# Mask weights of 128 columns, and filler products placed ahead of the evacuation of their bank, in a causal-attention and channel-mix kernel

## The chip, the cores and the metric

The kernel runs on one core of one Trainium2 chip. The metric is the device time of one execution in microseconds (us), and the median of the runs is compared. The engines are PE (TensorE, the matrix products; PEld is its weight loads, which overlap the products), DVE (VectorE), ACT (ScalarE), POOL (GpSimd) and SP, which issues the DMAs. PE reads weights and moving data from SBUF and writes to PSUM, which has eight banks. DVE and ACT read the results out of PSUM.

## The reference

Inputs are q, k and v for 4 batches and 12 heads, 448 positions, 64 values a head, and the weights of a channel mix.

```python
scores = scale * np.matmul(q, k.transpose(0, 1, 3, 2))
mask = np.triu(np.ones((seq, seq), dtype=bool), k=1)
scores = np.where(mask, -1000000000.0, scores)
scores = scores - np.max(scores, axis=-1, keepdims=True)
attn = np.exp(scores)
attn = attn / (np.sum(attn, axis=-1, keepdims=True) + 1e-09)
x = np.matmul(attn, v)                     # 12 heads side by side: 768 channels
...
xk = mu_k * x + (1.0 - mu_k) * x_prev      # x_prev: x one position back
xr = mu_r * x + (1.0 - mu_r) * x_prev
k = np.maximum(xk @ w_k, 0.0)              # 768 -> 1024
v = k * k @ w_v                            # 1024 -> 768
r = 1.0 / (1.0 + np.exp(-(xr @ w_r)))      # 768 -> 768
out = r * v
```

## The kernel before

**Tiling.** Two heads make a pair, and there are 24 pairs (w = 0 to 23), six in a batch. The 448 positions are cut into four chunks of 112. The scores of a pair are made in three groups (g = 0, 1, 2), and each group has one PSUM tile `s` of two banks, one bank for each head j. There are two such tiles (the ring `s`), so the scores of group g+2 wait until the exponentials of group g have been read out. The channel mix of a batch follows its six pairs: the products `mk` (with w_k), `mr` (with w_r) and `mv` (with w_v). The weights arrive from HBM during the first pairs and are taken apart into two halves on ACT, POOL and DVE (`wraw`, `wk`, `wr`, `wv`; lines L689, L699, L703).

**The mask as products.** In `score`, four small products (L381, a quartet: two column ranges h by two heads j) write the mask into the diagonal blocks before the score products (L394) add to it. Their weights are `pick`, a selection matrix of 64 rows by 112 columns for each h, their moving data is `mask`. Head j lies on partitions 64j to 64j+63 of both, so a product of j = 0 uses one half of the rows of PE's array and one of j = 1 the other half. A quartet has four weight loads of `pick`. There are 72 quartets, 288 mask products.

**The rest of a pair.** DVE takes the row maxima (`row_max`, L411; `row_top`, L425 or L423), ACT makes the exponentials (`exps`, L434), and in the first six pairs PE turns them (`turn_e`, L512, tiles `eT`) and DVE or ACT copies the turned blocks to SBUF (`copy_e`, L523, tiles `pT`). The `eT` tiles stand in the ring `s` for pairs 2 and 3 and in the ring `m` for pairs 0, 1, 4 and 5. The weighted sum (L554) goes into one PSUM tile `bank`, which is read by `evac` on DVE (L571), which multiplies it into `xt`. The row sums take a way of their own (`rs`, `rp`, `rt`, `sp`: L452, L459, L465, L469, L475, L485).

**The filler.** The function `idle` issues pairs of a weight load and a product that no result depends on (L277, weights `busy` of 128x128, 64 columns out). They are written into `spill`, the 64 columns of `bank` behind the 448 that hold the weighted sum, so that they share a tile with the reads of `evac`:

```python
bank = ps_x.tile([P, 512], F32, name="bank")
spill = bank[:, S:]
```

**The order.** Nothing is scheduled while the kernel runs. Every step is an `op` of a plan, and `Plan.run` issues all of them in the order of a table of numbers, `starts`. Each filler run is an entry `[number, pieces]` of the table `fills`, which is put among the steps by its number and issues twice as many products as it has pieces. An engine works through its own instructions in that order. A wait between engines is set where a later instruction of the order touches what an earlier one writes or reads: a filler issued behind an `evac` waits for that read, and an `evac` issued behind a filler waits for the filler.

Of the kernel before, what the change touches and what calls it, by code (L numbers as in the profile page):

```python
# [11 lines left out]
BF16 = mybir.dt.bfloat16  # L12
# [21 lines left out]
class Plan:  # L34
# [60 lines left out]
    "engines": "PPPPPPADADAAPPDADADADDPPDDDADDDDDDADAPDDDDDPAADADADADAADPPAAADDAAAADDDDPAADDADDADAPAADDDAADDPPPPPPDPDAPDDADDADDPADPDDPADPADPADAAADDADADDAAAADDADADADADADADDDDDADADDDADAPPDDDPDADDDADDDAAADAAPDPDADDDADDDADPDADADPDAPAADAAAPPAAAPDADAADPPDADPDDPDDAPPADAADADDDAAPDPPDPPPDDADDAAADAPDDAPADAAPAAPAPDAAADPPDAADADAADDDPADDDDADPPAAPDADAPPPPPADADAAAPADDDDPDPAAAAADAADDDAAAADADDDADADAPADADADAADADAAAAAAAPDDDAADDADADPPAADDADADDPAPAPADDPPPPDADDPDDDDDPPDDDDADDPPAAADDPAADDDDADADADDAPAAAPDDDADDDDDDDDDPDDPADADADPPPDDDADADDAAPDDDADPADAAAADADADDDDDADADDADDPADADPDADAPAAAAADAAAAAAAPADDAPDADDDPPAAAPAPAPPAADPPAADDDAPDDPPPPADPAPDDPDAAPDADDAPDADAPPDPDPDDDDADPPADDDDDPPPDPPDDAAAADPPADADPDAAPDPPPDDDAAADADDPDAPPADAAADDDDDADADAAADAPDDDDAPAPADDPDDADDD",  # L95
    "fills": [[5,12],[125,16],[295,12],[485,2],[1345,16],[1575,2],[1645,2],[1685,1],[2015,2],[2075,4],[2225,16],[2335,2],[2355,1],[2915,5]],
}
# [3 lines left out]
def tile_causal_attention_channel_mix(  # L101
# [10 lines left out]
    nc = tc.nc  # L112
    B, NPAIR, P, _, S = qk.shape
    D = P // 2
    DM, DFF = w_k.shape
    CP = 112
# [16 lines left out]
    const = ctx.enter_context(tc.tile_pool(name="const", bufs=1))  # L133
# [27 lines left out]
    def triangles(t, other, pattern, by, base, fill):  # L161
        for x, off in ((other, 0), (t, D)):
            nc.gpsimd.affine_select(
                out=x, in_=x, pattern=pattern, compare_op=ALU.is_ge,
                fill=fill, base=base - by * off, channel_multiplier=by,
            )

    pick = const.tile([P, 2, CP], BF16, name="pick")
    mask = const.tile([P, 2, 1, CP], BF16, name="mask")
    mask_up = parted(x_ts[-1][:, 1 : 1 + CP])  # L170
    cleared(pick, mask_up, mask)
    ident = const.tile([P, P], F32, name="ident")
    make_identity(nc, ident)
    triangles(mask, mask_up, [[D, 2], [0, 1], [-1, CP]], 1, 0, masked)
    nc.vector.tensor_copy(pick[:D, 0], ident[:D, :CP])
    nc.vector.tensor_copy(pick[D:, 0, :D], ident[D:, D:])
    nc.vector.tensor_copy(pick[:D, 1, D:], ident[:D, : CP - D])
    nc.vector.tensor_copy(pick[D:, 1, D:], ident[D:, D:CP])
    nc.vector.tensor_copy(mask[:D], mask_up[:D])  # L179
# [5 lines left out]
    for h in range(2):  # L185
# [5 lines left out]
            fill=1.0,  # L191
# [142 lines left out]
    def short(w):  # L334

        return CHOICE["short"][w] == "R"
# [30 lines left out]
    def score(w, g):  # L367

        s = ps_s.tile([P, 2, 512], F32, tag="s", name=f"s_{w}_{g}")
        sps[w, g] = s  # L370
        for h in (1, 0):
            for j in range(2):
                rows = slice(D * j, D * j + D)
                a = D * h
                if g == 0:
                    diagonal = s[:CP, j, :S].rearrange("p (a b) -> p a b", a=2)[:, :, a:CP]
                    fill = mask[rows, h, :, a:].to_broadcast([D, 2, CP - a])
                else:
                    (c,) = STEPS[g]
                    diagonal, fill = s[:CP, j, CP * c + a : CP * (c + 1)], mask[rows, h, 0, a:]  # L380
                nc.tensor.matmul(  # L381
                    diagonal, pick[rows, h], fill, start=h == 1, stop=False, skip_group_check=True
                )
        if short(w):
            hi, lo = qkh[w]
            products = [(hi, lo), (lo, hi), (hi, hi)]
        else:
            products = [(qkt[w], qkt[w])]
        for c, o in STEPS[g].items():
            n = CP * (c + 1)  # L390
            for i, (q_, k_) in enumerate(products):
                for j in range(2):
                    rows = slice(64 * j, 64 * j + 64)
                    nc.tensor.matmul(  # L394
                        s[:CP, j, o : o + n],
                        q_[rows, 0, c * CP : (c + 1) * CP],
                        k_[rows, 1, :n],
                        start=False,
                        stop=c == max(STEPS[g]) and i == len(products) - 1,
                        skip_group_check=True,  # L400
                    )
# [624 lines left out]
    def scores(w):  # L1026
        ts_, tu = ("st", w, 3), ("su", w, 2)
        if short(w):
            n = 2 * S
            raw, hi, lo = have["qk", w], ("qk", nexts("qk"), NQ), ("qk", nexts("qk"), NQ)  # L1030
            plan.op(copied(n), 0, qk_hi, (w,), [(raw, None, "r"), (hi, None, "w")], fast=True)
            plan.op(less(n), 0, qk_lo, (w,), [(raw, None, "r"), (hi, None, "r"), (lo, None, "w")], fast=True)
            parts = [(hi, None, "r"), (lo, None, "r")]
        else:
            parts = [(have["qk", w], None, "r")]
        for g, chunks in enumerate(STEPS):
            s = ("s", nexts("s"), NS)
            n = sum(CP * (c + 1) for c in chunks)
            plan.op(
                "PE", (3 if short(w) else 4) * n / 2.4 + (150 if g == 0 else 175), score, (w, g),  # L1040
                parts + [(s, None, "w")],
            )
            plan.op(
                "DVE", sum(dve(2 * CP * (c + 1)) for c in chunks) - 88 * (len(chunks) - 1), row_max, (w, g),
                [(s, None, "w"), (ts_, g, "w")],
            )
            plan.op({"ACT": 210, "DVE": 160}, 0, row_top, (w, g), [(s, None, "r"), (ts_, g, "w")])
            for c in chunks:
                for j in range(2):
                    te = ("e", 2 * w + j, NE)  # L1050
                    plan.op(
                        "ACT", scalar(CP * (c + 1), True, 1) + 85, exps, (w, g, j, c),
                        [(s, None, "r"), (ts_, g, "r"), (te, c, "w"), (tu, (j, c), "w")],
                    )
# [287 lines left out]
```

## Time and profile before

| | |
|---|---|
| three runs | 473.27, 475.01, 475.00 us, median 475.0 us |
| the profiled execution, time | 472.84 us |
| its span, first to last instruction | 471.1 us |
| PE busy | 458.3 us (97% of the span) |
| DVE, ACT, POOL busy | 355.7, 298.3, 169.6 us |
| mean granted clock of PE | 0.993 of full speed |

Times in the trace are counted from the start of the span. Between the span and the execution's time lie 1.7 us. Matmuls are pipelined and their ends are modelled, so the start of one matmul to the start of the next says more than the duration of either. The granted clock is given as a share: 1.00 is 2.4 GHz and 0.50 is 1.2 GHz.

### The profile page before, as it was taken

The page shows a single profiled execution, that of the slowest core. Times are in us where ns is not written, and L with a number is a line of the kernel's source. Part 1 is how long each engine was busy: PE and PEld are TensorE (multiplying, and loading weights), DVE is VectorE, ACT ScalarE, POOL GpSimd, SP SyncE. Part 2 cuts the span into 40 slices and gives each one's busy share as a digit, 9 for nine tenths or more (in the row PEclk, how much of TensorE's full clock was granted, in tenths as well). Part 3 has the DMA queues.
Part 4 walks back from the last instruction along what each step waited for, and adds up shares of the span by engine and source line. Part 5 has one row for each costly group of instructions (what it writes and reads, how often), then busy time and mean ns, then how long its engine had stood idle before and what let it go on. Part 6 is the DMA issues. An engine that isn't in the chain of part 4 may idle for free.

```text
span 471.1 us, 9420 instructions
## 1 busy us (share of the span) xinstructions
PE 458.3 (97%) x3565; PEld 268.0 (57%) x3565; DVE 355.7 (76%) x719; ACT 298.3 (63%) x821; POOL 169.6 (36%) x177
## 2 busy tenths in 40 slices
PE   8987999999999999999999999999999999999996
PEld 6655765554455656655566556555665655555553
DVE  5978799999898979989878999375689875434121
ACT  5978699999878958766657673655469543024200
POOL 4434354323121651353472343465413342124100
PEclk9989899999999999999999999999999999999999
DMA  8975575657046878183066399374155574000011
GB/s 309 323 285 202 180 248 174 186 210 176 0 101 120 185 135 157 60 212 92 1 118 139 87 168 213 76 173 88 34 95 109 105 131 129 1 0 1 0 61 58
DMA packets 94846, 60.59 MB, mean 129 GB/s; under 512 B 83408, under 2 KB 86480, under 8 KB 94032
## 3 DMA queue, kind: packets, MB, share of 16 engines
q1 hardware_dynamic: 94800, 59.98, 50.2%
q8 instruction: 28, 0.46, 0.4%
q14 instruction: 18, 0.15, 0.1%
HBM read 33.82 MB, written 5.51 MB: 83 GB/s over the span
## 4 chain that ended last, share of the span: by engine, by line
PE 80%; DVE 10%; ACT 4%; issue 2%; DMA 2%; POOL 1%; SPq 0%; DVEq 0%; ACTq 0%; POOLq 0%
PE mv L815 21%; PE mk L815 18%; PE mr L815 13%; PE s L394 7%; PE bank L554 6%; PE mk L830 4%; PE mr L830 3%; PE s L381 3%; DVE s L411 2%; PE eT L512 2%; ACT e L434 2%; DMA wraw<-in_w_k_dram 2%; PE sp L475 1%; DVE xr L598 1%; ACT junk L655 1%
## 5 line engine op out<-in xcount | busy, mean ns | idle before, releaser
L815 PE MATMUL mv<-k,wv 128*128 128x448 f16 x576 | 113.7, 353 | 0.0
L434 ACT ACTIVATE e<-s,st 112x336 f32<-112x336 f32 (+3 forms) x192 | 93.0, 493 | 21.4 <-DVE st L425 16.4
L815 PE MATMUL mk<-xk,wk 128*128 128x448 f16 x432 | 83.8, 353 | 0.0
L815 PEld LDWEIGHTS <-wv 128*128 128x128 f16 x576 | 54.7, 98 | 50.4 <-issue 2.0
L411 DVE TENSOR_REDUCE s<-s 112x2 f32<-112x224 f32 (+2 forms) x96 | 70.8, 745 | 12.3 <-PE s L394 9.3
L815 PEld LDWEIGHTS <-wk 128*128 128x128 f16 x486 | 46.6, 98 | 43.2 <-issue 1.2
L815 PE MATMUL mr<-xr,wr 128*128 128x448 f16 x270 | 55.2, 352 | 0.0
L815 PEld LDWEIGHTS <-wr 128*128 128x128 f16 x270 | 26.1, 99 | 23.2
L434 ACT ACTIVATION_READ_ACCUMULATOR e<-s,st 112x1 f32 x192 | 38.9, 203 | 0.0
L830 PE MATMUL mk<-xk,wk 128*128 128x448 f32 x96 | 37.7, 545 | 0.0
L925 DVE SCALAR_TENSOR_TENSOR a<-mv,kap,a 128x448 f32<-128x448 f32 x24 | 16.2, 680 | 26.8 <-PE mv L815 26.2
L492 DVE TENSOR_TENSOR p<-e,p 112x1120 f16<-112x1120 f32 x25 | 34.3, 1377 | 1.3 <-ACT p L488 1.2
L492 POOL TENSOR_TENSOR p<-e,p 112x1120 f16<-112x1120 f32 x11 | 26.7, 2430 | 18.8 <-ACT p L488 13.1
L554 PEld LDWEIGHTS <-vs 112*64 112x64 f16 x648 | 26.8, 110 | 6.2 <-issue 5.2
L830 PE MATMUL mr<-xr,wr 128*128 128x448 f32 x72 | 29.8, 550 | 0.0
L554 PE MATMUL bank<-pT,vs 112*64 112x224 f16 (+1 forms) x648 | 29.5, 245 | 0.0
L598 DVE SCALAR_TENSOR_TENSOR xf<-xt,shares,xf 128x448 f32<-128x448 f32 x36 | 25.1, 698 | 5.5 <-ACT xf L227 5.1
L699 POOL TENSOR_SCALAR wraw<-wraw 128x768 int32<-128x768 uint16 (+1 forms) x18 | 21.0, 1165 | 22.8 <-DMA wraw<-in_w_v_dram 12.5
L830 PEld LDWEIGHTS mk<-xk,wk 128*128 128x128 f32 x96 | 17.7, 190 | 16.9 <-issue 15.7
L838 ACT ACTIVATE a<-mk 128x448 f32<-128x448 f32 x18 | 9.8, 542 | 27.4 <-PE mk L815 26.3
L394 PE MATMUL s<-ql,qh 64*112 64x112 f32 (+3 forms) x144 | 25.7, 352 | 0.0
L381 PE MATMUL s<-mask,pick 64*112 64x48 bf16 (+3 forms) x288 | 22.9, 234 | 1.3 <-DVE mask L179 0.6
(219 smaller groups left out, 839.3 us busy)
## 6 DMA issues: line engine op xcount, KB each, us to landing
qk<-in_qk_dram SPq DMA_DIRECT2D x24, 448.0 KB, 4.0
wraw<-in_w_k_dram SPq DMA_DIRECT2D x6, 1024.0 KB, 8.5
wraw<-in_w_v_dram SPq DMA_DIRECT2D x8, 768.0 KB, 5.4
vraw<-in_v_dram SPq DMA_DIRECT2D x24, 224.0 KB, 4.6
out_dram<-a SPq DMA_DIRECT2D x24, 224.0 KB, 2.9
wraw<-in_w_r_dram SPq DMA_DIRECT2D x6, 768.0 KB, 4.4
pT<-p SPq DMA_TRANSPOSE x36, 4.7
muT<-in_mu_dram SPq DMA_DIRECT2D x1, 6.0 KB, 10.6
```

Of the source, the lines that this page charges most:

```text
L381: nc.tensor.matmul(diagonal, pick[rows, h], fill, start=h == 1, stop=False, skip_group_check=True)
L394: nc.tensor.matmul(s[:CP, j, o : o + n], q_[rows, 0, c * CP : (c + 1) * CP], k_[rows, 1, :n], start=False, stop=c == max(STEPS[g]) and i = ...
L411: nc.vector.tensor_reduce(most(w, g, c, c + 1), s[:CP, :, o : o + CP * (c + 1)], AX.X, ALU.max, negate=True)
L434: nc.scalar.activation(em[w, j][:, blocks(c)].rearrange("p a b -> p (a b)"), sps[w, g][:CP, j, o : o + CP * (c + 1)], AF.Exp, bias=stat[w] ...
L492: tt[e](p[:, NB:, :CP], em.pop((w, j)), p[:, :NB, :CP], ALU.subtract)
L554: nc.tensor.matmul(px[w][64 * j : 64 * j + 64, cols], value(j, vi), p(j, pi), start=n == 0 and i == 0, stop=last and i == len(steps) - 1, ...
L598: nc.vector.scalar_tensor_tensor(f, x_of(w)[:, :S], share(w, mu, 1), f, ALU.mult, ALU.add)
L699: nc.gpsimd.tensor_scalar(t, u, TOP3, -0.499, ALU.mult, ALU.add)
L815: nc.tensor.matmul(ps, w[:, wi, cols], x[:, xi, t0 : t0 + n], start=(i == 0 and a == 0), stop=(i == steps - 1 and a == 2),)
L830: nc.tensor.matmul(mps[m, kind, o][:, :n], z[:, o * P : (o + 1) * P], x, start=i == 0, stop=i == NO - 1)
L838: nc.scalar.activation(a, mps[m, "k", f][:, :n], AF.Relu)
L925: nc.vector.scalar_tensor_tensor(s, mps.pop((m, "v", o))[:, : M[m][2]], kap[m][:, 3:4], s, ALU.mult, ALU.mult)
```

## The change

The tile `pick` gets 128 columns in place of 112. The 16 new columns stay zero, so the mask products write 128 partitions of the scores in place of 112, and those 16 partitions are read by nobody. In `fills`, the run of 16 pieces at 1345 becomes one of 12 at 1245, the run of 16 pieces at 2225 is gone, and the last one has 3 pieces in place of 5: 44 filler products fewer, 142 in place of 186. `starts` and `engines` are the same. The number at the end of a tile's name differs between the two kernels, because names are counted as tiles are made.

```diff
-    "fills": [[5,12],[125,16],[295,12],[485,2],[1345,16],[1575,2],[1645,2],[1685,1],[2015,2],[2075,4],[2225,16],[2335,2],[2355,1],[2915,5]],
+    "fills": [[5,12],[125,16],[295,12],[485,2],[1245,12],[1575,2],[1645,2],[1685,1],[2015,2],[2075,4],[2335,2],[2355,1],[2915,3]],
...
-    pick = const.tile([P, 2, CP], BF16, name="pick")
+    pick = const.tile([P, 2, P], BF16, name="pick")
...
-    nc.vector.tensor_copy(pick[:D, 0], ident[:D, :CP])
+    nc.vector.tensor_copy(pick[:D, 0, :CP], ident[:D, :CP])
     nc.vector.tensor_copy(pick[D:, 0, :D], ident[D:, D:])
-    nc.vector.tensor_copy(pick[:D, 1, D:], ident[:D, : CP - D])
-    nc.vector.tensor_copy(pick[D:, 1, D:], ident[D:, D:CP])
+    nc.vector.tensor_copy(pick[:D, 1, D:CP], ident[:D, : CP - D])
+    nc.vector.tensor_copy(pick[D:, 1, D:CP], ident[D:, D:CP])
...
-                    diagonal = s[:CP, j, :S].rearrange("p (a b) -> p a b", a=2)[:, :, a:CP]
+                    diagonal = s[:, j, :S].rearrange("p (a b) -> p a b", a=2)[:, :, a:CP]
...
-                    diagonal, fill = s[:CP, j, CP * c + a : CP * (c + 1)], mask[rows, h, 0, a:]
+                    diagonal, fill = s[:, j, CP * c + a : CP * (c + 1)], mask[rows, h, 0, a:]
```

**First place.** These are PE's instructions of before around the run at 1345: the scores of group 1 of the fourth pair, a turned block, and the start of the filler run of 32 products, behind which the scores of group 2 (`s_2`) stand.

```order
L394 MATMUL s_1_524<-qk_434 112x336 x2
L512 MATMUL eT_1_2_535<-ident,e_1_344 112x112 [waits Activation_49]
L512 MATMUL eT_1_2_535<-ident,e_1_344 112x112 x3
L277 LDWEIGHTS busy
L277 MATMUL bank<-busy 128x64 [waits DVE_49]
```

These are PE's instructions of the changed kernel at the same place, ahead of a run of 24 products.

```order
L394 MATMUL s_1_524<-qk_434 112x336 x2
L512 MATMUL eT_1_2_535<-ident,e_1_344 112x112 [waits Activation_49]
L512 MATMUL eT_1_2_535<-ident,e_1_344 112x112 x3
L277 LDWEIGHTS busy
L277 MATMUL bank<-busy 128x64
```

On PE nothing has moved against its neighbours, since no step of PE stands between 1245 and 1345. The filler's wait for DVE is gone. On DVE the `evac` of that stretch (L571) stood without a wait before:

```order
L411 TENSOR_REDUCE s_1_524<-s_1_524 112x2 [waits PE_49,Activation_49]
L523 COPY pT_1_513<-eT_1_1_520 112x336
L425 TENSOR_SCALAR st_508<-s_1_524 112x2 [waits DVE_49]
L571 TENSOR_TENSOR xt_92<-bank,xt_92 128x448
L703 SCALAR_TENSOR_TENSOR wk<-wk,wraw_503 128x1024 [waits DMAHW2_49,Activation_49,Pool_49]
```

In the changed kernel DVE has the same rows, and the wait stands at the `evac`:

```order
L411 TENSOR_REDUCE s_1_524<-s_1_524 112x2 [waits PE_49,Activation_49]
L523 COPY pT_1_513<-eT_1_1_520 112x336
L425 TENSOR_SCALAR st_508<-s_1_524 112x2 [waits DVE_49]
L571 TENSOR_TENSOR xt_92<-bank,xt_92 128x448 [waits PE_49]
L703 SCALAR_TENSOR_TENSOR wk<-wk,wraw_503 128x1024 [waits DMAHW2_49,Activation_49,Pool_49]
```

The wait between filler and `evac` has changed its direction.

**Second place.** These are PE's instructions of before around the run at 2225: turned blocks of the fifth pair, the turned row sums `rp`, and the start of the second run of 32 products, behind which `eT_0_1_818` of the fourth pair stands.

```order
L512 MATMUL eT_0_0_768<-ident,e_0_706 112x112 x3
L512 MATMUL eT_0_1_774<-ident,e_0_706 112x112 x3
L465 LDWEIGHTS rs_136 [waits Pool_49]
L465 MATMUL rp_782<-identh,rs_136 128x112
L277 LDWEIGHTS busy
L277 MATMUL bank<-busy 128x64 [waits DVE_49]
```

In the changed kernel the next turned block of the fourth pair (`eT_0_1_778`) follows at once:

```order
L512 MATMUL eT_0_0_760<-ident,e_0_698 112x112 x3
L512 MATMUL eT_0_1_766<-ident,e_0_698 112x112 x3
L465 LDWEIGHTS rs_136 [waits Pool_49]
L465 MATMUL rp_774<-identh,rs_136 128x112
L512 MATMUL eT_0_1_778<-ident,e_0_517 112x112 [waits DVE_49,PE_49,Activation_49]
L512 MATMUL eT_0_1_778<-ident,e_0_517 112x112 x2
```

The wait for the `evac` is gone here with the run. No other engine has a row more or less, and apart from the filler PE has the same rows in the same order.

## Rows read from the trace of the kernel before

**Rows 1.** The page, part 1: busy time, share of the span, instructions.

```profile
PE 458.3 (97%) x3565; PEld 268.0 (57%) x3565; DVE 355.7 (76%) x719; ACT 298.3 (63%) x821; POOL 169.6 (36%) x177
```

**Rows 2.** Waits of PE over the span: us in total, times, longest.

```profile
PE bank L277 <- DVE xt L571: 4.9, 2, 2.9
...
PE bp_gm L260 <- DVE diag L256: 0.4, 1, 0.4
```

**Rows 3.** Timeline, first place: start, us, engine, line, shapes, count, [idle before].

```profile
25.40 0.59 PE L512 MATMUL eT<-ident,e 112*112 112x112 f32 x4
...
26.86 0.37 ACT L434 ACTIVATE e<-s,st 112x112 f32<-112x112 f32 x1
...
27.30 0.63 DVE L571 TENSOR_TENSOR xt<-bank,xt 128x448 f32<-128x448 f32 x1
...
27.83 1.23 DVE L703 SCALAR_TENSOR_TENSOR wk<-wk,wraw 128x1024 uint32<-128x1024 uint32 x1
...
27.98 1.87 PE L277 MATMUL bank<-busy 128*128 128x64 f16 x32 [1.99 <-DVE xt L571]
...
29.77 0.43 PE L381 MATMUL s<-mask,pick 64*112 64x48 bf16 x4
...
30.00 1.54 PE L394 MATMUL s<-qk 64*112 64x448 f32 x4
...
31.67 1.10 DVE L411 TENSOR_REDUCE s<-s 112x2 f32<-112x896 f32 x1 [2.62 <-PE s L394]
```

**Rows 4.** Timeline of PE at full clock: a filler run and a group 2 of scores.

```profile
10.70 0.86 PE L277 MATMUL bank<-busy 128*128 128x64 f16 x24
...
20.43 1.01 PE L394 MATMUL s<-qk 64*112 64x448 f32 x4
```

**Rows 5.** Windows: stretch, us, busy (count) of PE, PEld, DVE, ACT, POOL, clock, DMA, GB/s.

```profile
28.00:31.00 3.00, 3.00 (x40) 2.32 (x39) 1.06 (x1) 2.14 (x6) 1.83 (x1) 0.50 0.99 393
...
44.00:47.00 3.00, 0.15 (x6) 0.15 (x6) 2.80 (x3) 2.65 (x8) 1.70 (x2) 1.00 0.85 313
...
48.00:51.00 3.00, 3.00 (x26) 2.89 (x25) 2.57 (x5) 1.13 (x3) 0.00 (x0) 0.54 0.11 42
```

**Rows 6.** Timeline, second place.

```profile
44.55 0.63 ACT L434 ACTIVATE e<-s,st 112x448 f32<-112x448 f32 x1
...
46.18 0.61 DVE L571 TENSOR_TENSOR xt<-bank,xt 128x448 f32<-128x448 f32 x1
46.85 1.09 PE L277 MATMUL bank<-busy 128*128 128x64 f16 x32 [2.91 <-DVE xt L571]
...
48.29 2.09 DVE L523 COPY pT<-eT 112x336 f32<-112x336 f32 x4 [1.50 <-PE eT L512]
...
51.97 0.36 PE L381 MATMUL s<-mask,pick 64*112 64x96 bf16 x4
...
53.02 1.07 DVE L411 TENSOR_REDUCE s<-s 112x2 f32<-112x224 f32 x2 [1.26 <-PE s L394]
```

**Rows 7.** Groups of weight loads by form: busy us, mean ns, idle before.

```profile
L554 PEld LDWEIGHTS <-vs 112*64 112x64 f16 x648 | 26.8, 110 | 6.2 <-issue 5.2 <-ACT k L227 0.4 <-DVE k L902 0.4
...
L381 PEld LDWEIGHTS <-pick 64*112 64x112 bf16 x288 | 15.5, 128 | 14.7 <-issue 9.0 <-DVE st L425 0.7 <-PE mk L830 0.7
...
L475 PEld LDWEIGHTS <-sel 128*128 128x128 f16 x96 | 6.3, 100 | 5.1 <-issue 2.9
```

**Rows 8.** Timeline of PE, 199.04 to 199.05: into a quartet of masks.

```profile
198.74 0.35 PE L815 MATMUL mk<-xk,wk 128*128 128x448 f16 x1
199.02 0.25 PE L381 MATMUL s<-mask,pick 64*112 64x96 bf16 x2
```

**Rows 9.** Windows of line L381 alone in that quartet: PE, PEld, clock.

```profile
199.08:199.10 0.02, 0.02 (x2) 0.02 (x4) 1.00 0.00 0
199.10:199.12 0.02, 0.02 (x4) 0.02 (x4) 1.00 0.00 0
```

**Rows 10.** The chain that ended last: start, us, products of one kind.

```profile
192.28 6.81 PE mk L815 x36
```

## The prediction

> **What bounds the kernel now.** I read the page's busy times first, then what PE waits for, then the timeline of all engines around the two longest waits, the clock there, and last the weight loads and the products around one quartet of masks.
>
> PE is busy for 97% of the span [rows 1]. Busy time of PE is modelled, so this alone doesn't make PE the bound. The waits do: PE lost 4.9 us in two waits of its filler products for `evac`, and of what it waits for later than 58 us no entry is over 0.4 us [rows 2]. What makes PE earlier in the first 60 us therefore arrives at the end, as long as the engines that feed it become earlier too.
>
> At the first place PE is through with the turned block at 25.99 (25.40 and 0.59). The filler behind it waits until DVE has read `bank` at 27.93, runs 32 products to 29.77, and only then come the masks and scores of group 2 [rows 3]. DVE sits idle for 2.62 us until these scores are there [rows 3]. Meanwhile the granted clock has gone to 0.50, that is 1.2 GHz, after PE had stood still, and PE stays there from 28 to 31 us [rows 5]: the four score products take 1.54 us in place of 1.01 at 2.4 GHz [rows 3, 4].
>
> The second place is alike. The filler waits 2.91 us for the `evac` that ends at 46.79, the turned blocks behind it are late, DVE is idle for 1.50 us for them and for 1.26 us for the next scores [rows 6]. PE has stood still in most of 44 to 47, and from 48 to 51 the clock is 0.54 [rows 5]. In both places products that were to keep PE at work are what held it up.
>
> **First place, term 1.** Ahead of `evac` in the order, 24 filler products start at 25.99 and take 0.86 us [rows 3, 4], so they end near 26.9. That costs nothing, because the work that hides them is ACT's last exponential of group 0, which ends at 27.23 [rows 3] and frees the PSUM tile that `s_2` needs. Without that cover it would be 0.86 us. The new wait of `evac` for the filler is over at 26.9 too, ahead of the 27.30 at which DVE comes to it; behind it on DVE stand L703 and the row maximum, which would be delayed if the filler ended later. The masks of group 2 then start at about 27.3 in place of 29.77, 2.4 us earlier, and at 2.4 GHz the scores are through at about 28.5. DVE is at L703 until 29.06 (27.83 and 1.23), so its row maximum starts at 29.06 in place of 31.67: **2.6 us**. From here DVE, and not PE, hands on the gain, since exponentials and turned blocks follow from the row maximum. If the clock falls there as before, the scores are through at 29.1 and DVE's part stays the same, while the weighted sum behind them runs slowly until about 31: I estimate 1.9 us as the lower end. I take 2.6, since PE's idle time shrinks from 1.99 to about 0.4 us. The DMA engines are full from 28 to 31 us (0.99) [rows 5], so transfers under way can't land sooner; but none of these rows waits for a DMA, so I count no loss.
>
> **Second place, term 2** (in times of before; all of it comes 2.6 earlier). The turned block behind the removed run needs a PSUM tile that ACT frees at 45.18 (44.55 and 0.63), not the `evac` [rows 6]. So PE goes on at 45.3 in place of 47.9. DVE still has its `evac` until 46.79 and copies the block at once, at 46.85 in place of 48.29: 1.4 us on DVE. Copies on DVE and ACT then free the tiles one after the other for the rest of the turned blocks, which at 2.4 GHz brings PE to the next masks at about 49.4 in place of 51.97. DVE's next row maximum starts at 50.4 in place of 53.02, 2.6 us. If PE runs at 1.2 GHz here, as it did from 48 to 51, the turned blocks and row sums there take about a microsecond more, and 1.4 us are left. With the run gone, PE is at work for under half of this stretch, and it fell to 1.2 GHz once with the filler, so I take **2.1 us** between 1.4 and 2.6.
>
> The four products fewer of the last run are worth 4 times 28 ns, 0.1 us at most, since the run of 24 has 28 ns between starts (0.86 less the 0.2 of one product, over 23) [rows 4]. I count nothing for them: PE waits there for copies anyway.
>
> **Mask weights, term 3.** The load of `pick` with 112 columns takes 128 ns, one of 64 columns 110, but one of 128 columns (`sel`) takes 100 [rows 7]. The stream shows it more clearly: filler products with a 128-column load each start every 28 ns [rows 4], so such a load takes at most 28 ns of the stream. In the quartet at 199.02 the third mask starts between 199.10 and 199.12, 80 to 100 ns behind the first [rows 8, 9]. The masks ahead of it have 96 columns, 41 ns at the 189 ns that 448 columns take (6.81 us over 36) [rows 10]. Some 40 to 60 ns are the wait for the second pair of loads, and a load of 28 ns would save about 20 there and as much again ahead of the score products. I take 45 ns for a quartet. It counts only where PE comes from other work than scores, whose longer products hide the loads, and where PE is the bound: I choose 30 of the 72 quartets, **1.3 us**. The bounds: 72 times 60 ns is 4.3 us; and if the load isn't faster, 16 columns more at the 0.4 ns a column between 64 and 112 columns (18 ns over 48) [rows 7] are 6 ns a load, 1.8 us lost over 288. I take the gain because the nearest row (`sel`, the same width and element size) has it, though with 128 rows.
>
> The Trainium skill has a rule against this term: "TensorE: Matmul & The Clock Gate", section "LDWEIGHTS (loading the stationary operand)", has a load's time grow with its columns; its formula gives, as an estimate, 93 ns for 112 and 107 for 128. By that the change would cost 14 ns a load, 4 us in all if none were hidden. The trace doesn't agree, since its 128-column loads are the shorter ones. The same page, section "Weight-path perf modes — Fast Weight Load (FWL) and DoubleRow", says why: a fast load is used when the weights are exactly 128 columns and not FP32. No row here shows it for weights of 64 rows.
>
> **The sum.** 2.6 + 2.1 + 1.3 = 6.0 us. From the profiled execution, 472.84, that gives 466.8. The median of the runs is 475.0, 2.2 above it, with a lowest run of 473.27. I put the sum between, as the wait for a clock that falls now and then may be part of that spread: **468.0 us**.
>
> **The rivals.**
> (a) The waits go, but the mask loads gain nothing or lose: the short load isn't to be had with weights of 64 rows. For it speaks that no 64-row load of 128 columns stands in the trace. 1.3 to 3.1 us less gain: 469.5 to 471, the waits alone giving 4.7. By the skill's rule on columns it would come out here.
> (b) The early gain is lost again: DVE's copies and row maxima, or weights that arrive no sooner, hold PE by 60 us, and only half of term 1 is left with term 3, 2.6 us: 472.5 or, from the median without the clock's part, up to 474. For it speaks that DVE and ACT are nearly full in that stretch; against it that DVE itself had 5.4 us idle at these two places for PE, and its work moves along.
> (c) Slower: a short load of 128 columns takes all of PE's way for weights and can't stand beside a running product of the other half of the rows. On the switch from full products to half rows PE shows 0.28 us where 0.19 is normal, 94 ns of standing still [rows 8, 10]. Paid at each of 288 loads that is 27 us, 468 plus 28, about 496; it decides from 25 ns a load on, 7 us, which eats terms 1 and 2 and the margin. Against it: 28 ns a load and product in the filler.
> (d) More: 72 quartets gain 60 ns and the second place its 2.6 us, 3.5 us more: 464.5.
>
> **How the numbers follow.** Forecast 58%, with its own range of 466 to 470; (a) 20%; (b) 11%; (c) 5%; (d) 6%. The range of 464.5 to 472.0 holds forecast, (a) and (d) and leaves out (c) and most of (b). A change of under 0.5%, 2.4 us, can't be told from none here: faster means below 472.6. Forecast, (a) and (d) are faster, and a part of (b): 0.86. The rest of (b) is 0.09 with no change, (c) is 0.05 slower.
>
> **What would show it.** In the changed kernel's profile PE has no wait of L277 for L571 at 27 or 46 us; the filler run starts at 26.0 and the masks of group 2 at 27.3; DVE's row maximum comes at 29.1; the clock is 1.00 from 28 to 31. The masks that stood at 51.97 start at about 47. Loads of `pick` have a mean near 100 ns, and the third mask of a quartet starts 50 to 60 ns behind the first. It would be wrong if a wait of another engine stands where the filler waited, if the clock stays at 0.50 from 44 us on, if loads of `pick` are at 128 ns or more, or if mask to mask grows.

## The result, and the profile after

The changed kernel takes **468.38 us** in the median of 4 runs (466.07 to 469.34), against 475.0 us before (473.27 to 475.02): a ratio of 0.986, with an interval of 0.982 to 0.991. The profiled execution took 467.75 us, with a span of 466.0 us and a mean granted clock of 0.999. That is 5.1 us less than the profiled execution of before, 472.84. The forecast was 468.0.

The page's busy times, which answer to [rows 1], and what PE waits for, which answers to [rows 2]:

```profile
PE 452.7 (97%) x3521; PEld 260.7 (56%) x3521; DVE 355.6 (76%) x719; ACT 298.1 (64%) x821; POOL 169.6 (36%) x177
```

```profile
PE s L381 <- ACT e L434: 2.2, 3, 1.0
PE eT L512 <- ACT e L434: 2.2, 4, 1.3
PE bank L273 <- DVE busy L148: 1.1, 1, 1.1
PE s L381 <- DVE wz L703: 1.0, 1, 1.0
PE eT L512 <- DVE pT L523: 0.8, 1, 0.8
```

PE no longer has the entry of 4.9 us, the filler's waits for `evac`. New ones stand in the list, of 1.3, 1.0, 1.0 and 0.8 us. Those of 1.3 and 0.8 us stand at the second place, where PE now comes ahead of ACT and DVE; those of 1.0 us stand at 104 and 141 us. The one of 1.1 us (L273) is at the very start and stood there before.

The timeline of the first place, which answers to [rows 3]:

```profile
25.56 0.86 PE L277 MATMUL bank<-busy 128*128 128x64 f16 x24
...
27.28 0.25 PE L381 MATMUL s<-mask,pick 64*128 64x48 bf16 x4 [0.86 <-ACT e L434]
27.36 0.98 PE L394 MATMUL s<-qk 64*112 64x448 f32 x4
...
27.17 0.62 DVE L571 TENSOR_TENSOR xt<-bank,xt 128x448 f32<-128x448 f32 x1
27.70 1.23 DVE L703 SCALAR_TENSOR_TENSOR wk<-wk,wraw 128x1024 uint32<-128x1024 uint32 x1
28.84 1.10 DVE L411 TENSOR_REDUCE s<-s 112x2 f32<-112x896 f32 x1
```

The filler runs at once, the masks of group 2 wait 0.86 us for ACT's last exponential, and DVE goes from L703 to its row maximum without a pause. The second place, which answers to [rows 6]:

```profile
42.43 0.93 PE L512 MATMUL eT<-ident,e 112*112 112x112 f32 x7 [1.32 <-ACT e L434]
...
44.38 0.50 PE L512 MATMUL eT<-ident,e 112*112 112x112 f32 x3 [0.83 <-DVE pT L523]
...
46.32 0.31 PE L381 MATMUL s<-mask,pick 64*128 64x96 bf16 x4
...
43.30 0.61 DVE L571 TENSOR_TENSOR xt<-bank,xt 128x448 f32<-128x448 f32 x1
43.84 1.85 DVE L523 COPY pT<-eT 112x336 f32<-112x336 f32 x4
...
47.33 1.07 DVE L411 TENSOR_REDUCE s<-s 112x2 f32<-112x224 f32 x2 [0.27 <-PE s L394]
```

The masks that stood at 51.97 start at 46.32, and DVE's row maximum comes at 47.33 in place of 53.02. The windows of [rows 5] again, with busy times of PE, PEld, DVE, ACT and POOL, the granted clock, the DMA share and GB/s:

```profile
28.00:31.00 3.00, 2.84 (x30) 1.84 (x29) 3.00 (x7) 2.79 (x8) 2.22 (x3) 1.00 0.97 388
44.00:47.00 3.00, 2.62 (x32) 2.32 (x34) 3.00 (x8) 2.08 (x7) 0.00 (x0) 1.00 0.47 184
48.00:51.00 3.00, 3.00 (x36) 1.89 (x34) 2.71 (x6) 2.59 (x10) 2.86 (x3) 1.00 0.82 306
```

The clock stays at 1.00 in all three. The loads of `pick`, which answer to [rows 7], and the mask quartet that stood at 199.02, as in [rows 8, 9] (PE and PEld of line L381 alone, clock):

```profile
L381 PEld LDWEIGHTS <-pick 64*128 64x128 bf16 x288 | 9.7, 95 | 19.1 <-issue 12.1 <-DVE st L425 0.7 <-PE mk L830 0.7
```

```profile
194.75 0.31 PE L381 MATMUL s<-mask,pick 64*128 64x96 bf16 x4
```

```profile
194.78:194.80 0.02, 0.02 (x2) 0.02 (x4) 1.00 0.00 0
194.80:194.82 0.02, 0.02 (x4) 0.02 (x4) 1.00 0.00 0
```

A load of `pick` takes 95 ns where it took 128, and the third mask starts 50 to 70 ns behind the first, where it was 80 to 100.

**Where the time came from.** The start of the same instruction in both traces: the masks of [rows 3] come 2.49 us earlier (27.28 for 29.77; 0.22 of it was there at the quartet ahead, 24.33 for 24.55), those of [rows 6] 5.65 earlier (46.32 for 51.97), and a mask quartet later on 5.94 earlier (94.24 for 100.18). Then some of it goes: the quartet at 140.79 stood at 144.83, 4.04 earlier. At the end of the span it is 5.1 us. Two of these quartets in the trace of before, and the first of them in that of the changed kernel (the other is shown in the last section):

```profile
100.18 0.27 PE L381 MATMUL s<-mask,pick 64*112 64x48 bf16 x4
...
144.83 0.27 PE L381 MATMUL s<-mask,pick 64*112 64x48 bf16 x4
```

```profile
94.24 0.25 PE L381 MATMUL s<-mask,pick 64*128 64x48 bf16 x4
```

Below, the lead of a kernel at a quartet is the time by which its masks start there earlier than in the trace of before.

### The profile page after: what moved, and what is told of

The parts are those of the page before. It is cut to its first block, busy times and chain, and to the rows that moved or that the text cites. A ratio compares the mean times of both kernels' runs of the same rounds, so it can differ in the third digit from the quotient of the medians.

```text
span 466.0 us, 9334 instructions
## 1 busy us (share of the span) xinstructions
PE 452.7 (97%) x3521; PEld 260.7 (56%) x3521; DVE 355.6 (76%) x719; ACT 298.1 (64%) x821; POOL 169.6 (36%) x177
## 4 chain that ended last, share of the span: by engine, by line
PE 72%; DVE 10%; ACT 10%; issue 3%; DMA 3%; POOL 1%; ACTq 0%; DVEq 0%; SPq 0%
PE mv L815 20%; PE mk L815 18%; PE mr L815 13%; PE s L394 6%; PE bank L554 6%; PE mk L830 4%; ACT e L434 4%; DVE s L411 3%; DMA pT<-p 2%; PE s L381 2%; ACT junk L655 1%; PE mr L830 1%; PE eT L512 1%; PE sp L475 1%; DVE wv L733 1%
## 5 line engine op out<-in xcount | busy, mean ns | idle before, releaser
L434 ACT ACTIVATE e<-s,st 112x336 f32<-112x336 f32 (+3 forms) x192 | 93.1, 495 | 18.4 <-DVE st L425 11.2
L434 ACT ACTIVATION_READ_ACCUMULATOR e<-s,st 112x1 f32 x192 | 39.3, 205 | 0.0
L492 DVE TENSOR_TENSOR p<-e,p 112x1120 f16<-112x1120 f32 x25 | 35.1, 1406 | 2.4 <-ACT p L488 2.4
L492 POOL TENSOR_TENSOR p<-e,p 112x1120 f16<-112x1120 f32 x11 | 26.9, 2444 | 19.5 <-ACT p L488 10.8
L488 ACT CAST p<-e 112x1120 f16<-112x1120 f32 x19 | 21.4, 1127 | 5.2 <-DMA pT<-p 2.7
```

Of the source, the lines that this page charges most:

```text
L434: nc.scalar.activation(em[w, j][:, blocks(c)].rearrange("p a b -> p (a b)"), sps[w, g][:CP, j, o : o + CP * (c + 1)], AF.Exp, bias=stat[w] ...
L488: copy[e](p_t[at_][:, :NB, :CP], em[w, j])
L492: tt[e](p[:, NB:, :CP], em.pop((w, j)), p[:, :NB, :CP], ALU.subtract)
```

## The experiments

All ratios are to the kernel before, run on the same chip, where its medians were 474.3 to 474.7 us. A ratio is worked out over the runs and can be up to 0.0015 off the quotient of the two medians. Of each kernel with 112 columns `pick` is that of before.

**One half alone.** The weights of 128 columns with the old fills, and the new fills with the old weights; the diffs are the two halves of the one shown above.

> The kernel before with the 128-column weights of the masks and its own filler runs. Theory (the waits carry the gain, the mask loads add a little): 1.3 us faster, between 0.5 and 2.5 (ratio 0.995 to 0.999); the filler still waits 4.9 us for the two evacuations; loads of pick near 95 ns. Rival M (the mask loads carry most of it and the early gain is lost downstream): 4 us or more faster (0.992 or less).

Measured: 473.32 us, 0.9965 (0.9939 to 0.9991), as expected. In its trace the two waits are still there, 5.1 us in total, and a load of `pick` takes 95 ns.

> The kernel before with the new table of filler runs and 112-column weights. Theory: both waits gone, 5.6 us earlier at the first masks behind the second place, and 4 to 5.5 us faster at the end (0.988 to 0.9915). Rival N (what counts is that there are 44 products fewer): 1.2 us at 28 ns each, up to 2.5 us at the rate of 58 ns at 1.2 GHz. Rival M: 1 to 2 us.

Measured: 473.44 us, 0.9973 (0.9952 to 0.9994). That is 1.3 us where 4 to 5.5 were expected, and in the range of rival M. In its trace both waits are gone, but the masks behind the second place have a lead of 3.0 us (48.95), not of 5.6: 1.0 us was lost ahead of the first place, and the clock was at 0.51 from 46 to 49 us. The two halves add up to 0.994, the whole change was 0.986. Either the halves help each other, or one of these numbers doesn't stand for what it was taken to stand for.

**One place alone.** The first edit of `fills` alone, then the removed run alone.

```diff
-[1345,16],
+[1245,12],
```

> The kernel before with the first run alone put ahead of its evacuation (12 pieces at 1245 in place of 16 at 1345): 8 products fewer. Theory: 2.6 to 2.8 us earlier behind the first place, the second wait stays at about 2.9 us, and 2 to 2.8 us faster at the end. Rival N: 8 products, 0.2 to 0.5 us.

Measured: 472.89 us, 0.9970 (0.9942 to 0.9997).

```diff
-[2225,16],
```

> The kernel before with the second run alone taken out (16 pieces at 2225): 32 products fewer. Theory: first wait stays at about 2.0 us, 2.1 to 2.8 us earlier at the masks behind the second place, 1.5 to 2.8 us faster at the end, with the clock at 1.00 or falling there as the term assumed. Rival N: 32 products, 0.9 us at 28 ns to 1.9 us.

Measured: 473.67 us, 0.9973 (0.9951 to 0.9995). In both traces the place that was edited gives what the theory said: the lead grows by 2.5 us at the first place and by 2.2 at the second, both more than rival N allows. But both times fell by less than expected. The first kernel loses 1.4 us of its lead between 207 and 285 us, the second 2.5 between 72 and 79 and 2.0 between 144 and 199, more than it had gained. Two edits that by their ratios give 1.4 and 1.3 us alone, and 1.3 together, can't be read as a sum.

**The change a second time**, beside the next three kernels.

> The changed kernel once more, with more runs, beside the next three. The two halves alone gave 0.9965 and 0.9973, together 0.9938 if they add up, and the changed kernel gave 0.9862 with four runs. Theory A (they add up, and the four runs were good ones): 0.991 to 0.995. Theory B (the halves help each other: the early gain of the runs is lost later when mask loads are slow, and kept when they are short): 0.985 to 0.989.

Measured: 469.59 us (466.52 to 473.26), 0.9894 (0.9852 to 0.9936). That is just above the range of B, and 0.994 just outside the interval; over both measurements, 0.988, it is B's number. Whether the halves help each other, as B says, the times alone don't show. Its profiled execution was a long one, with a span of 471.5 us. These rows of its trace say where it lost, the windows with the same columns as above:

```profile
75.84 1.86 PE L830 MATMUL mk<-xk,wk 128*128 128x448 f32 x2 [2.17 <-DVE xk L598]
```

```profile
45.00:48.00 3.00, 3.00 (x26) 2.64 (x24) 2.19 (x6) 2.50 (x7) 0.56 (x2) 0.51 0.37 102
76.00:79.00 3.00, 3.00 (x12) 1.17 (x12) 2.93 (x6) 1.49 (x7) 1.83 (x2) 0.50 0.22 90
```

PE stood still for 2.17 us where the first execution of the same kernel had no wait, and twice the clock was at 0.50 where it had been 1.00. At the second place its lead grows by 1.5 us less than in the first execution, and around 76 us it loses another 3.9: together 5.4 of the 5.5 us between the two spans.

**Are the products fewer, or earlier?** All 186 products kept, with the three later runs ahead of the evacuations; then the changed kernel without the run at 1245.

```diff
-[1245,12],[1575,2],[1645,2],[1685,1],[2015,2],[2075,4],[2335,2],[2355,1],[2915,3]
+[1245,16],[1575,2],[1645,2],[1685,1],[2015,2],[2075,4],[2195,16],[2335,2],[2355,1],[2915,5]
```

> The changed kernel with all 186 filler products of before, both long runs ahead of their evacuations in the order (16 pieces at 1245, 16 at 2195, 5 at 2915). Theory (the waits carry the early gain, not the number of products): the masks behind the second place start within 0.6 us of the changed kernel's (46.3), and the time is within 0.4% of it. Rival N (the number of products): 44 products more cost 1.2 to 2.5 us there.

Measured: 467.82 us, 0.9866 (0.9828 to 0.9904). The time is as expected. The masks behind the second place start at 47.75, not within 0.6 us of 46.3 but 1.4 later; 1.3 of that was there ahead of the first place (25.63 for 24.33), and from there on the two differ by 0.1 us.

```diff
-[1245,12],
```

> The changed kernel without the run at 1245: 24 products fewer. Theory: they stood in time in which PE waits for ACT, so the scores of group 2 start at 27.3 as in the changed kernel and the early part is the same, unless the clock falls to 1.2 GHz behind 1.6 us of standing still, as it did before; then 0 to 1.5 us are lost by the masks at 46.3. Rival: fewer products are faster by themselves, 0.7 us.

Measured: 468.34 us, 0.9863 (0.9837 to 0.9888). As expected, the scores of group 2 start at 27.33, the masks behind the second place at 46.09, and the clock stays at 1.00. With all 186 products, 142 or 118 the time is the same within the intervals, about 2 us, and what the two places give differs by 0.1 and 0.3 us from the changed kernel: it is the place that counts there, not the number.

**Exactly 128?** The changed kernel with weights of 120 columns.

```diff
-    pick = const.tile([P, 2, P], BF16, name="pick")
+    pick = const.tile([P, 2, 120], BF16, name="pick")
...
-                    diagonal = s[:, j, :S].rearrange("p (a b) -> p a b", a=2)[:, :, a:CP]
+                    diagonal = s[:120, j, :S].rearrange("p (a b) -> p a b", a=2)[:, :, a:CP]
```

> The changed kernel with mask weights of 120 columns. Theory (exactly 128 columns make the load short): loads of pick at about 128 to 131 ns as with 112 columns, the third mask 75 to 90 ns behind the first, and 1 to 1.5 us slower than the changed kernel. Rival (more columns than 112 are enough, or the count of partitions written matters): loads near 97 ns and the same time.

Measured: 473.70 us, 0.9978 (0.9953 to 1.0003), the same as the new fills with 112 columns, and 4.1 us slower than the changed kernel beside it where 1 to 1.5 were expected. Its weight loads:

```profile
L381 PEld LDWEIGHTS <-pick 64*120 64x120 bf16 x288 | 16.2, 131 | 17.2 <-issue 12.0 <-PE mk L830 0.7 <-DVE wz L703 0.7
```

With 120 columns a load takes 131 ns, more than with 112 (128). Behind full products the third mask starts 83 ns after the first (the median of 16 quartets; 86 before, 52 in the changed kernel). Of the three widths tried, only 128 has the short load.

**Is the rest lost in collisions?** With the new fills and slow loads (112 or 120 columns), and in the changed kernel without the run at 1245, PE waited 1.2 us near 285 us. In the last one the timeline around it reads:

```profile
279.41 2.57 DVE L355 SCALAR_TENSOR_TENSOR vs<-vraw,vsc,vs 112x512 f16<-112x512 f32 x1
...
279.14 2.29 POOL L345 TENSOR_TENSOR ql<-qk,qh 128x896 fp32r<-128x896 f32 x1 [6.59 <-ACT qh L340]
...
282.57 0.21 PE L465 MATMUL rp<-identh,rs 112*128 112x112 f16 x1 [1.20 <-DVE xt L485]
```

DVE's L355 starts 0.27 us after GpSimd's L345 and takes 2.57 us in place of the 0.75 of the kernels without this wait. To take this away, the cast that releases GpSimd is put behind another one on ScalarE, in two kernels. On ACT, against the kernel without the run:

```order
-L340 CAST qh_3802<-qk_3593 128x896
-L605 CAST xk_3806<-xf_15_3716 128x448
+L605 CAST xk_3802<-xf_15_3716 128x448
+L340 CAST qh_3804<-qk_3593 128x896
```

> The new filler runs with the 112-column mask weights, and one more edit: on ScalarE the cast of xk at L605 stands ahead of the cast of qh at L340 where the kernel with the fills alone lost 1.2 us (PE waited there for DVE xt L485). In that kernel GpSimd's ql at L345 started 0.27 us ahead of VectorE's vs at L355, and that L355 took 2.57 us instead of 0.75. Theory C (collisions: what the two halves lack of the whole is lost later, in places where the engines that follow meet each other at a worse moment): L355 is back at 0.75 us, the wait of 1.2 us and the 0.4 us behind it are gone, and the time falls by 1.2 to 1.6 us against the fills alone, to a ratio of about 0.993 to 0.995 against the kernel before. Theory L (the 112-column loads themselves eat the gain, and any wait that is taken away comes back elsewhere): the ratio stays at 0.997.

> The change without its filler run at 1245, which showed the same stretched L355 (2.57 us) and the same wait of 1.2 us, with the same swap on ScalarE (L605 ahead of L340). Theory C: the wait goes, the time falls by 1.2 to 1.6 us, from a ratio of 0.986 to about 0.983, which would be the fastest version. Theory L: 0.986, since the wait comes back elsewhere.

Measured: 472.91 us, 0.9964 (0.9934 to 0.9994), and 468.82 us, 0.9878 (0.9834 to 0.9922). In the second one's trace:

```profile
281.82 0.74 DVE L355 SCALAR_TENSOR_TENSOR vs<-vraw,vsc,vs 112x512 f16<-112x512 f32 x1
...
284.57 1.46 DVE L609 TENSOR_TENSOR xk<-xf,xk 128x448 f16<-128x448 f32 x1
...
283.47 2.08 POOL L345 TENSOR_TENSOR ql<-qk,qh 128x896 fp32r<-128x896 f32 x1 [8.53 <-ACT qh L340]
...
287.87 0.31 PE L381 MATMUL s<-mask,pick 64*128 64x96 bf16 x4 [0.66 <-DVE st L425]
```

L355 is back at 0.74 us and PE's wait of 1.20 is gone. GpSimd's L345 now meets DVE's L609 instead (1.46 us), and a wait grows from 0.18 to 0.66. So the place gave back part of what it cost, as theory C says, but the time didn't fall as it said. In the first one's trace L355 is back at 0.74 us too, but at 69 us DVE's L703 takes 3.10 us in place of 0.95, and PE waits 1.4 us behind it. Up to 280 us both kernels have the order of the kernels they are made from, and yet the executions differ ahead of it: the second starts its masks of group 2 at 28.64 where the kernel it is made from had 27.33, and waits 1.1 us at 105 us for L703 in place of 0.3. What one execution loses at such places changes from run to run by more than the 1.2 us of this one.

**Other fills with the slow loads.** The two filler lists of above that gave 0.9866 and 0.9863, now with 112 columns.

> All 186 filler products, the three later runs ahead of the evacuations of their bank, with the mask weights of 112 columns of the kernel before. Theory C: the early gain of 5 to 6 us is kept less the collisions of this order's own timing, which need not be those of the fills alone: a ratio of 0.987 to 0.993, near 1.2 us (the mask loads) above the same fills with 128 columns, which gave 0.9866. Theory L: as with the changed kernel's fills and 112 columns, 0.996 to 0.998, whatever the fills.

> The changed kernel's fills without the run at 1245, with the mask weights of 112 columns. Theory C: 0.987 to 0.993, by the collisions of its own timing; the same fills with 128 columns gave 0.9863. Theory L: 0.996 to 0.998.

Measured: 469.68 us, 0.9904 (0.9869 to 0.9939), and 470.96 us, 0.9907 (0.9871 to 0.9943). This is theory C's expectation, and theory L falls: slow loads don't eat the gain of the fills. It is with the list of the change itself that most of it is lost when the loads are slow. In the waits of PE of the first of the two kernels (the trace is of its fastest execution, 467.71 us)

```profile
PE eT L512 <- ACT e L434: 1.2, 3, 0.4
PE bank L273 <- DVE busy L148: 1.1, 1, 1.1
PE eT L512 <- DVE pT L523: 0.8, 1, 0.8
PE s L381 <- ACT e L434: 0.7, 2, 0.4
```

no entry but the one at the very start (L273) reaches a microsecond, while the new fills alone have

```profile
PE s L381 <- ACT e L434: 2.5, 3, 1.4
PE eT L512 <- ACT e L434: 2.1, 3, 1.4
PE rp L465 <- DVE xt L485: 1.2, 1, 1.2
```

The second of the two kernels has the stretched L355 and PE's wait near 285 us as well (1.1 us), one of 1.1 us at 106, and 1.4 and 1.6 at the first two places, and still 0.9907: the waits of one execution don't account for a median.

## Why the prediction was right, point by point

**Term 1, first place: 2.6 us forecast.** From the quartet ahead of it to the one behind it the lead grows by 2.6 us (0.22 to 2.83), and by 2.5 to 2.7 in each of the eleven traces in which this run is moved or gone; in the two others it is 0.1. DVE's row maximum came 2.83 earlier (28.84 for 31.67). The filler's end is hidden by ACT's exponential, as it was said, and the clock did not fall. The step held. That PE waits for another engine where the filler had waited, a sign against the forecast by its letter, is the cover that the term had counted on (ACT's exponential, 0.86 us here, 0.4 forecast). The kernel without this run has the same time within the intervals, so nothing shows that the 24 products there need be at all.

**Term 2, second place: 2.1 us chosen, between 1.4 and 2.6.** It was 2.8 us: 5.65 at the masks of 46.32, of which the first place and the start had brought 2.84 by then. PE's wait of 1.32 us there is for the tile that ACT frees, as the term had it. The size was off because I let the clock fall there; in this execution it stayed at 1.00. Of the ten traces with both places edited, seven have the clock at 1.00 there and gain 2.8 to 3.2 us; in three, the second profiled execution of the change among them (0.51 from 45 to 48), it fell and they gain 1.4 to 2.2. So the lower bound was right, and the upper one 0.2 to 0.6 us too low.

**Term 3, the mask weights: 1.3 us.** The mechanism was right: a short load is to be had for weights of 64 rows, and rivals (a) and (c) fall. The traces show it apart from everything else. From 60 us on, the lead of each of the six kernels traced with 128 columns grows by 20 to 120 ns at 30 to 33 of the quartets; with its smaller steps that makes 1.6 to 1.7 us. In the seven traces with 112 or 120 columns that growth is between -0.1 and 0.1 us (the losses at single places are left out in both). So the count of 30 quartets was right, and 45 ns for each of them a little low, since 1.3 us stand against some 1.65. With the filler list held the same, 128 columns gave 0.9965 alone, 0.9866 for 0.9904, and 0.9863 for 0.9907: 1.7, 1.8 and 2.1 us of 474, with intervals of 1.2, 2.5 and 2.1 to either side. The Trainium skill, "TensorE: Matmul & The Clock Gate", section "Weight-path perf modes — Fast Weight Load (FWL) and DoubleRow", asks for exactly 128 columns; the trace agrees, with 131 ns at 120 columns and 95 at 128.

**What the sum left out: losses later on.** The three terms gave 7.2 us in the trace (2.6, 2.9 by the second quartet behind the second place, 1.7) where the sum had 6.0, and 2.4 us went again behind 94 us. That is rival (b), at later places than I had put it, and the sum had nothing for it: DVE's L703 holds PE for 1.0 us at 104, and the exponentials of L434 hold it for 1.0 at 141. The sentence that what makes PE earlier in the first 60 us arrives at the end was too strong. But these losses don't come from PE being early. The kernel with 128 columns and the old fills is 1.1 us behind the kernel before at that point and waits as long for L703; the kernel without the run at 2225 alone is 0.65 us behind and waits as long for L434:

```profile
111.07 0.22 PE L381 MATMUL s<-mask,pick 64*128 64x96 bf16 x2 [1.08 <-DVE wz L703]
```

```profile
146.69 0.26 PE L381 MATMUL s<-mask,pick 64*112 64x48 bf16 x3 [1.04 <-ACT e L434]
```

All products ahead with 112 columns, with a lead of 5.4 us, waits 0.4 us for L703 and not at all at 141, and 5.1 us of it arrive. The wait at 141 goes with the number of products, as the last section shows; that at 104, of 1.0 to 1.1 us, stands in six of the 14 traces, with 128 columns and with 112, and what decides it is open.

The total came out right in part by luck. Terms that were 1.2 us too small and losses of 2.4 that were left out make 5.1 us in the traces where the sum had 6.0, and the forecast of 468.0 had been put 1.2 above the 466.8 of the sum for the clock. The second measurement gave 469.59.

**Why the halves don't add up.** With the list of the change, 112 and 120 columns gave 0.9973, 0.9978 and 0.9964, and 128 columns 0.9862 and 0.9894, 4.4 us apart; with the two other lists the columns are worth 1.8 to 2.1. So an excess of about 2.5 us, with an interval of 2.0 to either side, belongs to this list with slow loads. Of it the traces show a wait of 1.3 to 1.4 us at 142 to 145 us and one of 0.4 at 182 to 186 in all three slow kernels, and in neither of the two with other lists: they cost 2.2 to 2.4 us of lead. The first also stands, with 1.0 us, in both traces of the change, where it costs 1.1 to 1.2; the last section says where it is from. So 1.1 us of the excess stand in every trace. The rest differs between the three traces (the clock at 0.50 from 45 us in two, stretched DVE instructions at 70 or 285 us) and stays open.

**How much is the clock.** In the 8 of 81 executions of before with a mean granted clock of 0.998 or more, the span has a median of 470.6 us, against 472.7 over all 81. For the change, measured twice, and its three variants with 128 columns it is 466.0 in 16 executions of 28, against 466.9 over all. So at a full clock the change is worth some 4.6 us, and the falls that it avoids add about 1.3, by estimate: executions picked by their clock may differ in other things too. One such thing is the start. The filler run of 32 products near 6.7 us takes 1.89 us in six of the 14 traces, where products still start at half the later rate, and 1.28 to 1.73 in the other eight; at 12.5 us those six are 0.5 to 1.1 us behind the trace of before, the others at most 0.3.

## What to carry to other kernels

A product that is to keep PE at work must not wait for anyone: one that writes a bank waits for every evacuation of that bank which stands ahead of it in the order, and may stop PE for longer than the pause that it was to fill. Weights can be padded to exactly 128 columns where the padding is free, also when they have 64 rows. And where executions lose 1 to 4 us at places that the change doesn't touch, a single pair of kernels, or of traces, can be off by as much: test the parts of a change against more than one version of the rest, and follow the lead over the whole span, where a part that acts everywhere shows as steady growth and a loss as a step.

## What the runs showed of the hardware that was not expected

**An instruction block among transposes.** The wait for L434 at 141 us goes back to a DMA. In the changed kernel ACT's cast of the probabilities waits for transposes that still read its buffer, and PE waits behind ACT:

```profile
136.93 1.12 ACT L488 CAST p<-e 112x1120 f16<-112x1120 f32 x1 [2.46 <-DMA pT<-p]
...
140.79 0.25 PE L381 MATMUL s<-mask,pick 64*128 64x48 bf16 x4 [1.04 <-ACT e L434]
```

The first of these transposes is issued at 130.93 and done 5.98 us later; in the kernel with all products ahead it takes 4.69. The DMA view of the changed kernel from 132.1 us, when its packets begin, to its landing at 136.91, in 40 slices (busy tenths, GB/s), with the queues below:

```profile
DMA  5999999999999700000100000899999999930029
GB/s 143 275 287 292 287 294 285 268 251 245 402 170 47 2 0 0 0 0 2 9 9 9 9 11 11 175 287 292 287 292 339 265 272 281 266 13 11 9 51 277
...
q8 instruction: 1, 0.02, 1.3%
```

The same view of the kernel with all products ahead, from 133.6 to 137.16:

```profile
DMA  1899999999999999999999997445899999712699
GB/s 43 193 282 291 288 296 285 291 293 288 285 268 276 253 247 288 293 270 227 247 242 219 244 239 176 90 141 121 187 230 265 262 196 95 49 20 20 52 181 259
...
q14 instruction: 1, 0.01, 0.5%
```

In the changed kernel a packet of the DMA queue q8, 0.02 MB of instructions, comes in the middle of the transpose, and for 1.4 us next to nothing moves. In the other the block has come before the transpose starts. All 14 traces of changed kernels and of before divide in this way: in the six whose filler list is that of the change, or lacks the run at 2225 alone, the block falls between the first packet and the landing, and the transpose takes 5.98 to 6.45 us; in the other eight it doesn't, and it takes 4.07 to 4.78. The six lose 1.1 to 1.6 us of their lead from one quartet to the next there, and no other changed kernel loses any, from 1.9 us behind the kernel before to 6.1 ahead of it. Which list has it is fixed by the number of products ahead (142 and 154 have it, 118, 178 and 186 don't), as it would be if the block is PE's own next instructions; the trace doesn't name the engine, and no run moved the block alone. The Trainium skill, "Runtime: NRT & Kernel Launch", section "Instruction fetch mechanics", has instructions come in blocks of 16 KiB at a cost that is mostly hidden. The 0.02 MB agree; the cost was not hidden here, where PE waits 1.0 us behind a transpose that the block fell into.

**DVE behind GpSimd.** DVE's L355 took 2.57 us when it started 0.27 us after GpSimd's L345, and 0.75 when it started first; the second profiled execution of the change shows the same with other instructions, and the first one the other order of the same two:

```profile
69.28 3.03 DVE L703 SCALAR_TENSOR_TENSOR wz<-wz,wraw 128x768 uint32<-128x768 uint32 x1 [0.18 <-ACT wraw L697]
...
69.19 2.31 POOL L492 TENSOR_TENSOR p<-e,p 112x1120 f16<-112x1120 f32 x1 [2.58 <-DVE p L488]
```

```profile
66.86 0.96 DVE L703 SCALAR_TENSOR_TENSOR wz<-wz,wraw 128x768 uint32<-128x768 uint32 x1
...
66.91 3.09 POOL L492 TENSOR_TENSOR p<-e,p 112x1120 f16<-112x1120 f32 x1 [3.87 <-DVE p L488]
```

Behind GpSimd L703 takes 3.03 us, ahead of it 0.96, and then GpSimd's L492 takes 3.09 for 2.31, and PE's wait of 2.17 us at 75.84 stands behind the long one. A tenth of a microsecond at the start of two instructions decides over 2 us. The Trainium skill, "SBUF — State Buffer", section "SBUF: two separate sides", says that the two engines share a pair of ports which the first to start holds for its whole instruction, if DVE's has two inputs in SBUF and GpSimd's reads SBUF. These rows agree roughly: the stretched instructions end 0.55 and 0.81 us behind GpSimd's, and take 0.75 and 0.95 alone. It is one reason why executions of one kernel differ.
